# In-place transposes queued one tile later, a weight narrowing queued behind the exponentials, and the last keys' transposes queued behind the scores, in a fused attention and two-layer MLP kernel

## The chip, the core and the metric

The kernel runs on one core of a Trainium2 chip. The metric is the device time of one execution in microseconds (us); lower is better. The engines are TensorE (PE, with its weight loads shown apart as PEld), VectorE (DVE), ScalarE (ACT), GpSimd (POOL) and SyncE (SP), whose queue here issues almost all DMAs. Each engine works through one queue of instructions in the order in which they stand in it.

## What is computed

```python
# attention: q, k, v are 4 x 8 x 576 x 64 (batch, heads, positions, head size), float32
q_rot, k_rot = rotate(q), rotate(k)                    # rotary embedding
scores = matmul(q_rot, k_rot.T) / sqrt(64)
attn = exp(scores - max(scores))
attn = attn / (sum(attn) + 1e-9)
x = matmul(attn, v)                                    # -> 2304 x 512
# first layer, d_ff 768
h = maximum(maximum(x @ w1, x @ w2), x @ w3)
y = h @ w_out
# second layer, d_ff 2048
h2 = y @ w_in
out = (h2 * sigmoid(h2)) @ w_out2
```

The weights come as 64-bit floats, the rest as float32.

## The kernel before

The attention goes through 80 **tiles**, 20 for each of the four batches b. A tile is the key (b, hp, t): hp is one of four pairs of heads, and t one of five blocks of queries. Tiles with t from 0 to 3 hold 128 queries of both heads of the pair, tiles with t = 4 hold the last 64 queries of both heads on one set of 128 rows. A batch is taken in two halves: first t = 0, 1 for each pair, then t = 2, 3, 4.

For the tile of number j the loop in `attention()` writes down, in this order:

- `tile_scores(j)`: PE multiplies queries by keys into the one score buffer `s` (lines 394 to 404). There is a single such buffer, so the next tile's scores wait until this tile's exponentials have read it.
- `tile_max(j)`: DVE takes the negated row maximum `nb` (line 414), ACT the exponentials `e` with their sums (line 421).
- `tile_flip` of an earlier tile, from batch 1 on (line 491): DVE transposes 32 x 32 blocks of `pt` in place, once the DMAs of that tile have brought the exponentials there. I call this the flip.
- `av` (lines 532 and 536) for a group of two or three tiles whose flips are done: PE multiplies by v into `xp`, and ACT and DVE split the result into `x` (lines 539, 540).
- `tile_norm(j - 1)`: ACT passes the sums on (line 430), DVE takes reciprocals `rec` (line 431), ACT scales the exponentials (line 433).
- `tile_move(j - 1)`, from batch 1 on: SP issues four DMAs from `e` to `pt` (line 471).
- `tile_last(j - 2)`, from batch 1 on: PE transposes the last keys' columns of `e` (lines 438, 439, 481), which ACT and DVE copy out. Batch 0 makes all its transposes on PE in `tile_turn` and has neither moves nor flips.

Beside each tile other work is written down. The first layer, `moe1`, is paced by `x_ready`: PE multiplies x by w1, w2, w3 and then by w_out (line 623) into two PSUM buffers `m`, which ACT and DVE empty (lines 639, 641, 647, 648, 665). The rotary steps of the next batch run on POOL (lines 330 to 334). And `narrow_w2` brings the second layer's weights from 64 to 32 bits in 64 pieces: SP loads piece n (line 805) into one of three `z64` buffers; `narrow_a` takes it one step later, on ACT (line 214) and on POOL (line 216); `narrow_b` takes both results on DVE (lines 225, 226), one step later again; then ACT measures the piece (line 140) and SP stores it (line 781). Beside it, and mostly in the later part of this stretch, `prep_w8` loads stored pieces again (line 912), combines them on POOL (line 888) and splits them on ACT and DVE (lines 892, 896).

What stands in an engine's queue, and in which order, is settled when the program is built: a scheduler lays the instructions of each engine out by times that it reckons for them, and `tc.issue_after(x)` ties the instructions traced inside it behind instruction x, if they are on x's engine. On another engine the tie does nothing. `last["max"]` is the newest row maximum, on DVE; `exps[-1]` the newest exponential, on ACT.

Of the kernel before, what the change touches and what calls it, by code (L numbers as in the profile page):

```python
# [17 lines left out]
P = 128  # L18
# [4 lines left out]
def fused_kernel(  # L23
# [22 lines left out]
    nc = tc.nc  # L46
# [37 lines left out]
    ident = const.tile([P, P], F32, name="ident")  # L84
# [164 lines left out]
    last = {}  # L249
# [87 lines left out]
    def moved(b):  # L337
        return b > 0
# [41 lines left out]
    s_t, e_t, sum_t, pt_t, exps = {}, {}, {}, {}, []  # L380
# [3 lines left out]
    def both(s, o, step, n):  # L384

        return bass.AP(tensor=s.tensor, offset=s.offset + o, ap=[list(s.ap[0]), [step, 2], [1, n]])
    evacs = [0]

    def tile_scores(key):
        b, hp, t = key  # L390
        T, K, Q = T_t[b, hp]
        s = ps_s.tile([P, 1536], F32, tag="s", name="s")
        if t == 4:
            nc.tensor.matmul(s[:, 0:512], Q, T[:, 512:1024], start=True, stop=True)
            nc.tensor.matmul(s[:, 512:576], Q, T[:, 1024:1088], start=True, stop=True)
            s_t[key] = s
            return
        n = P
        qs = T[:, t * P:t * P + n]
        kt = T[:, 512:1024]  # L400
        nc.tensor.matmul(both(s, 512, 448, 64), qs, K, start=True, stop=True)  # L401
        for g, o in ((0, 0), (1, 1024)):
            r = slice(64 * g, 64 * g + 64)
            last["s"] = nc.tensor.matmul(s[:, o:o + 512], qs[r], kt[r], start=True, stop=True).ins  # L404
        s_t[key] = s

    def heads(key):
# [27 lines left out]
    def turn_last(e, to):  # L435

        tr = ps_t.tile([P, 512], F32, tag="tr", name="tr")
        nc.tensor.transpose(tr[:, 0:P], e[:, 448:576], ident)
        nc.tensor.transpose(tr[0:64, P:2 * P], e[:, 512:576], ident)
        to = to.rearrange("p (i q) -> p i q", i=2)  # L440
        t4 = tr[:, 0:2 * P].rearrange("p (a q i g) -> p a g i q", a=2, g=2, i=2)
        nc.scalar.activation(out=to[0:64], in_=t4[0:64, 1, 0], func=AF.Copy)
        nc.vector.tensor_copy(out=to[64:128], in_=t4[64:128, 0, 1])
# [29 lines left out]
    def tile_last(key):  # L473

        e = e_t.pop(key)
        pt, o = pt_of(key)
        to = blocks(pt)[1]
        if key[2] == 4:
            return turn_last(e, to[:, o:o + 64])
        tr = ps_t.tile([P, 512], F32, tag="tr", name="tr")  # L480
        nc.tensor.transpose(tr[:, 0:P], e[:, 512:640], ident)
        nc.scalar.activation(
            out=to[:, o:o + P].rearrange("p (i q) -> p i q", i=4), in_=tr[:, 0:P].rearrange("p (q i) -> p i q", i=4), func=AF.Copy
        )

    def tile_flip(key):

        pt, o = pt_of(key)
        n = 2 if key[2] == 4 else 4
        x = blocks(pt)[0][:, o // 32:o // 32 + n].rearrange("p i c k -> p (i c k)")  # L490
        nc.vector.transpose(out=x, in_=x)  # L491

    def tile_turn(key):
        b, hp, t = key
# [55 lines left out]
    tiles, events, first, x_ready, av_at = [], {}, {}, {}, {}  # L550

    def at(j, f, *a):
        events.setdefault(j, []).append((f, a))

    for b, hp, r in order:
        first.setdefault((b, hp), len(tiles))
        tiles += [(b, hp, t) for t in PARTS[r][2]]
        av_at.setdefault(len(tiles) + (3 if moved(b) else 2), []).append((b, hp, r))
        x_ready[b, r] = len(tiles) + (5 if moved(b) else 4)
    for i, (b, hp) in enumerate(pairs):  # L560
        u = first[b, hp]
        if b > 1:
            j = first[b, 0] + 3 * hp - 7
# [10 lines left out]
    for b in range(1, B):  # L574
        u = first[b, 0]
        for hp in range(NP):
            at(u - 10 + hp if hp < 2 else u - 3, load_v, b, hp)
            at(u - 6 + hp + hp // 2 * 2, v_max, b, hp)
        at(u, v_scale, b)

    def attention():

        back = lambda j, n: tiles[j - n] if n <= j < len(tiles) + n else None
        for j in range(len(tiles) + 5):
            if j < len(tiles):
                tile_scores(tiles[j])
                tile_max(tiles[j])
            key = back(j, 3)
            if key and moved(key[0]):
                tile_flip(key)  # L590
            for a in av_at.pop(j, ()):
                av(*a)
            key = back(j, 1)
            if key:
                tile_norm(key)
                if moved(key[0]):
                    tile_move(key)
            key = back(j, 2)
            if key:
                (tile_last if moved(key[0]) else tile_turn)(key)  # L600
            for f, a in events.pop(j, ()):
                f(*a)
            yield
# [165 lines left out]
    def narrow_w2(W, src, nm):  # L769

        part = {}
        M = W.m * 512 // 256
        for n in range(M + 4):
            if n >= 4:
                W.measure(n - 4)
                if nm == "wi":
                    i, o = divmod(n - 4, 2)
                    q, c = divmod(i, KC)  # L780
                    nc.sync.dma_start(
                        out=zscr[nm].rearrange("p (f c n) -> p f c n", c=KC, n=P)[:, 4 * q + 2 * o:4 * q + 2 * o + 2, c],
                        in_=W.t[n - 4].rearrange("p (f n) -> p f n", n=P),
                    )
                else:
                    nc.sync.dma_start(out=zscr[nm][:, (n - 4) * 256:(n - 3) * 256], in_=W.t[n - 4])
            if 2 <= n <= M + 1:
                with tc.issue_after(last["max"]):
                    W.narrow_b(n - 2, part.pop(n - 2, None))
            if 1 <= n <= M:  # L790
                if wide:
                    W.t[n - 1] = z_p.tile([P, 256], F32, tag="z", name="z")
                with tc.issue_after(last["max"]):
                    W.narrow_a(n - 1, part.get(n - 1), pool=True)
            if n < M:
                i, o = divmod(n * 256, 512)
                if nm == "wi":
                    q, c = divmod(i, KC)
                    from_ = src[c * P:(c + 1) * P, q * 512 + o:q * 512 + o + 256]
                else:  # L800
                    from_ = src[i * P:(i + 1) * P, o:o + 256]
                if wide:
                    part[n] = z64_p.tile([P, 256], w1.dtype, tag="z64", name="z64")
                    with tc.issue_after(last["load"]):
                        nc.sync.dma_start(out=part[n], in_=from_)
                else:
                    W.t[n] = z_p.tile([P, 256], F32, tag="z", name="z")
                    nc.sync.dma_start(out=W.t[n], in_=from_)
            yield
        W.scale("s" + nm, n=M)  # L810
        yield
# [572 lines left out]
```

## Time and profile before

| | us |
|---|---|
| median of 3 runs | 1084.35 (1081.48 to 1087.41) |
| profiled execution | 1086.89 |
| its span, first to last instruction | 1085.1 |
| PE busy | 941.8 (87%) |
| DVE busy | 690.9 (64%) |
| ACT busy | 606.9 (56%) |
| POOL busy | 493.3 (45%) |

The profile lists for each group of instructions how long it was busy, how long its engine stood idle just before it, and what ended that idle time. Busy shares are means over stages: batch 0's attention (to 165 us), attention of batches 1 to 3 beside the first layer (165 to 675), the end of the first layer (to some 740), and the second layer.

### The profile page before, as it was taken

To read this page: it belongs to the slowest core of one execution; us is meant where nothing else is said; L and a number is where in the kernel's file an instruction comes from. 1 tells how busy PE (TensorE), PEld (TensorE's weight loads), DVE (VectorE), ACT (ScalarE), POOL (GpSimd) and SP (SyncE) were. 2 spreads that over 40 slices of the span, in tenths; PEclk is the share of its full clock that TensorE was granted. 3 is DMA by queue.
4 is the path that set the end of the run, shared out by engine and by line. 5 is a ranking of instruction groups with operands and counts; after the bars stand their busy time and mean duration, and the time that the engine had idled before them with its cause. 6 is when DMAs were issued, how large, how long until landed. Compare 5 with 4: busy or idle time off the path is not lost. (4 is left out here: it accounts for less than half of the span.)

```text
span 1085.1 us, 19113 instructions
## 1 busy us (share of the span) xinstructions
PE 941.8 (87%) x6802; PEld 678.6 (63%) x6802; DVE 690.9 (64%) x1231; ACT 606.9 (56%) x1381; POOL 493.3 (45%) x548
## 2 busy tenths in 40 slices
PE   4677998888877978877978878999999899999998
PEld 2343664554554544454554446768888788888887
DVE  5658888544567544576655664576478677666554
ACT  3778686534665654566665654355455455545442
POOL 6734694850335600163132220276358646647254
PEclk9687998899999999998999898999999999999999
DMA  6833146755777855678677874635445234433201
GB/s 158 254 110 97 40 123 110 166 102 99 170 143 155 170 108 90 145 195 214 153 183 165 179 190 69 196 116 183 141 145 176 88 122 141 122 123 122 69 21 40
DMA packets 185198, 146.29 MB, mean 135 GB/s; under 512 B 51216, under 2 KB 168720, under 8 KB 185104
## 3 DMA queue, kind: packets, MB, share of 16 engines
q1 hardware_dynamic: 183600, 144.36, 53.5%
q8 instruction: 54, 0.88, 0.4%
q10 hardware_dynamic: 1504, 0.72, 0.2%
q14 instruction: 40, 0.33, 0.1%
HBM read 90.51 MB, written 26.21 MB: 108 GB/s over the span
## 5 line engine op out<-in xcount | busy, mean ns | idle before, releaser
L623 PE MATMUL m<-x,w 128*128 128x256 f16 (+1 forms) x1388 | 208.9, 300 | 23.0 <-DVE t L641 14.7
L623 PEld LDWEIGHTS <-w 128*128 128x128 f16 x1632 | 162.8, 102 | 100.9 <-issue 53.2
L216 POOL TENSOR_SCALAR z<-z 128x256 uint16<-128x256 uint16 x64 | 51.5, 804 | 242.0 <-ACT z L214 232.8
L491 DVE STREAM_TRANSPOSE pt<-pt 128x1024 f32<-128x1024 f32 (+1 forms) x60 | 68.2, 1137 | 140.5 <-DMA pt<-e 140.4
L1110 PEld LDWEIGHTS <-g 128*128 128x128 f16 x1485 | 146.1, 98 | 17.6
L1047 PEld LDWEIGHTS <-w8s 128*128 128x128 f16 x1344 | 131.1, 98 | 16.1 <-issue 0.9
L421 ACT ACTIVATE e<-s,nb 128x576 f32<-128x576 f32 x144 | 105.0, 734 | 54.7 <-DVE nb L414 53.7
L433 ACT ACTIVATE e<-e,rec 128x576 f32<-128x576 f32 x144 | 104.1, 766 | 53.1 <-DVE rec L431 52.8
L888 POOL TENSOR_TENSOR z<-z 128x128 f32<-128x128 f32 (+1 forms) x96 | 63.3, 677 | 102.1 <-PE m L120 46.3
L414 DVE TENSOR_REDUCE nb<-s 128x2 f32<-128x1152 f32 (+1 forms) x80 | 98.2, 1227 | 15.4 <-PE s L404 14.6
L536 PE MATMUL xp<-pt,vd 128*64 128x256 f32 (+1 forms) x512 | 83.0, 422 | 6.0 <-DVE pt L491 3.4
L404 PE MATMUL s<-T 64*128 64x512 f32 x256 | 84.4, 740 | 0.0
L1061 POOL TENSOR_TENSOR z<-t 128x256 f32<-128x256 f32 x32 | 27.1, 847 | 88.9 <-DVE t L1053 54.0
L623 PE MATMUL m<-h,wo 128*128 128x256 f16 (+1 forms) x448 | 66.0, 294 | 1.6 <-DVE wo L163 1.5
L214 ACT ACTIVATE z<-z 128x256 f32<-128x256 f32 x64 | 27.5, 431 | 69.3 <-DMA z<-in_moe_w_out_dram 41.8
L623 PEld LDWEIGHTS <-wo 128*128 128x128 f16 x512 | 50.6, 100 | 22.9 <-issue 8.0
L999 DVE SCALAR_TENSOR_TENSOR g<-gsum,sg,g 128x1024 f16<-128x1024 f32 x36 | 49.1, 1372 | 23.7 <-ACT g L998 23.3
L536 PEld LDWEIGHTS xp<-pt,vd 128*64 128x64 f32 x512 | 35.8, 138 | 41.5 <-issue 14.7
L998 ACT ACTIVATE g<-gsum,sg 128x1024 f16<-128x1024 f32 x36 | 40.8, 1141 | 36.9 <-POOL gsum L994 36.9
L330 POOL TENSOR_TENSOR w<-qk,sin_sb 128x384 f32<-128x384 f32 (+1 forms) x44 | 45.5, 1057 | 20.0 <-DMA qk<-in_q_dram 10.3
L401 PE MATMUL s<-kd,T 128*128 128x128 f32 x128 | 31.1, 329 | 23.4 <-ACT e L421 21.7
L1110 PE MATMUL c<-w,g 128*128 128x256 f16 x376 | 48.9, 277 | 0.0
(248 smaller groups left out, 1978.4 us busy)
## 6 DMA issues: line engine op xcount, KB each, us to landing
w8s<-w8scr SPq DMA_DIRECT2D x64, 448.0 KB, 4.4
pt<-e SPq DMA_DIRECT2D x192, 128.0 KB, 3.9
z<-in_moe_w_in_dram SPq DMA_DIRECT2D x32, 256.0 KB, 3.7
z<-in_moe_w_out_dram SPq DMA_DIRECT2D x32, 256.0 KB, 3.5
w<-in_moe_w_dram SPq DMA_DIRECT2D x6, 768.0 KB, 6.5
wo<-in_moe_w_dram SPq DMA_DIRECT2D x6, 768.0 KB, 4.8
qk<-in_q_dram SPq DMA_DIRECT2D x32, 128.0 KB, 3.8
vd<-in_v_dram SPq DMA_DIRECT2D x16, 256.0 KB, 3.2
```

What stands on the lines that cost most here:

```text
L216: nc.gpsimd.tensor_scalar(out=q[:, :, 2], in0=q[:, :, 1], scalar1=step, scalar2=off, op0=ALU.mult, op1=ALU.add)
L404: last["s"] = nc.tensor.matmul(s[:, o:o + 512], qs[r], kt[r], start=True, stop=True).ins
L414: x = nc.vector.tensor_reduce(out=nb[:, 0:m], in_=both(s, 0, 960, 576) if m > 1 else s[:, 0:576], op=ALU.max, axis=AX.X, negate=True)
L421: x = nc.scalar.activation(out=e[:, HK[g]], in_=s[:, SK[g]], func=AF.Exp, bias=nb[:, g:g + 1], accum_out=sm[:, g:g + 1])
L433: nc.scalar.activation(out=e[:, HK[g]], in_=e[:, HK[g]], func=AF.Copy, scale=r[:, g:g + 1])
L491: nc.vector.transpose(out=x, in_=x)
L536: nc.tensor.matmul(xp[r, 0:n], v4[:, g, c, :], turned(c, g), start=False, stop=(c == 3))
L623: nc.tensor.matmul(ps[:, 0:n], l, r, start=(first and i == 0), stop=(not more and i == len(passes) - 1))
L888: nc.gpsimd.tensor_tensor(out=z[:, o], in0=z[:, x], in1=z[:, y], op=op)
L999: nc.vector.scalar_tensor_tensor(out=l, in0=x, scalar=sg_t[jb], in1=h, op0=ALU.mult, op1=ALU.subtract)
L1047: nc.tensor.matmul(o, l, r, start=(i == 0), stop=(i == len(passes) - 1))
L1110: x = nc.tensor.matmul(ps, l, r, start=first, stop=last_, skip_group_check=True)
```

## The change

- The flip is tied behind `last["max"]`, and it is written down for tile j - 2 instead of j - 3. As it is traced after `tile_max(j)`, that is the maximum of the second next tile.
- `narrow_a` in `narrow_w2` is tied behind `exps[-1]`. Before, it named `last["max"]`, a DVE instruction, which ties nothing on ACT or POOL.
- PE's transposes of the last keys are tied behind the newest score matmul, now kept in `last["score"]`.
- The moved batches lose the extra step: `av` is written down two steps behind its last tile instead of three, `x_ready` is four instead of five, and the loop ends a step earlier. The loads of v for two head pairs go one step earlier.

```diff
@@ tile_scores
-            nc.tensor.matmul(s[:, 512:576], Q, T[:, 1024:1088], start=True, stop=True)
+            last["score"] = nc.tensor.matmul(s[:, 512:576], Q, T[:, 1024:1088], start=True, stop=True).ins
...
-            last["s"] = nc.tensor.matmul(s[:, o:o + 512], qs[r], kt[r], start=True, stop=True).ins
+            last["s"] = last["score"] = nc.tensor.matmul(s[:, o:o + 512], qs[r], kt[r], start=True, stop=True).ins
@@ turn_last
-        nc.tensor.transpose(tr[:, 0:P], e[:, 448:576], ident)
-        nc.tensor.transpose(tr[0:64, P:2 * P], e[:, 512:576], ident)
+        with tc.issue_after(last["score"]):
+            nc.tensor.transpose(tr[:, 0:P], e[:, 448:576], ident)
+            nc.tensor.transpose(tr[0:64, P:2 * P], e[:, 512:576], ident)
@@ tile_last
-        nc.tensor.transpose(tr[:, 0:P], e[:, 512:640], ident)
+        with tc.issue_after(last["score"]):
+            nc.tensor.transpose(tr[:, 0:P], e[:, 512:640], ident)
@@ tile_flip
-        nc.vector.transpose(out=x, in_=x)
+        with tc.issue_after(last["max"]):
+            nc.vector.transpose(out=x, in_=x)
@@
-        av_at.setdefault(len(tiles) + (3 if moved(b) else 2), []).append((b, hp, r))
-        x_ready[b, r] = len(tiles) + (5 if moved(b) else 4)
+        av_at.setdefault(len(tiles) + 2, []).append((b, hp, r))
+        x_ready[b, r] = len(tiles) + 4
...
-            at(u - 10 + hp if hp < 2 else u - 3, load_v, b, hp)
+            at(u - 10 + hp if hp < 2 else u - 4, load_v, b, hp)
@@ attention
-        for j in range(len(tiles) + 5):
+        for j in range(len(tiles) + 4):
...
-            key = back(j, 3)
+            key = back(j, 2)
@@ narrow_w2
-                with tc.issue_after(last["max"]):
+                with tc.issue_after(exps[-1]):
                     W.narrow_a(n - 1, part.get(n - 1), pool=True)
```

The first place is DVE's queue in batch 1, from the maximum of tile 29 (counted from 0) to that of tile 30, whose line has only one pair of results less (128x1). Before, the rows are these; the flip of `pt` is that of tile 28, and `rec_2498` is tile 29's reciprocal.

```order
L414 TENSOR_REDUCE nb_2399<-s_2395 128x2
L225 TENSOR_SCALAR z_2357<-z_2357 128x256
L491 STREAM_TRANSPOSE pt_2423<-pt_2423 128x1024
L226 SCALAR_TENSOR_TENSOR z_2357<-z_0_2287,z_2357 128x256
L641 SCALAR_TENSOR_TENSOR t_2469<-m_2456,t_2454 128x320
L540 SCALAR_TENSOR_TENSOR x_2094<-xp_2544,vs_1706,x_2094 128x256
L431 RECIPROCAL rec_2498<-rec_2498 128x2
L414 TENSOR_REDUCE nb_2492<-s_2489 128x1
```

In the changed program the same two maxima are followed by these rows of DVE; the first flip is tile 27's, the second tile 28's, and `rec_2511` is tile 29's reciprocal.

```order
L414 TENSOR_REDUCE nb_2412<-s_2408 128x2
L494 STREAM_TRANSPOSE pt_2262<-pt_2262 128x1024
L225 TENSOR_SCALAR z_2370<-z_2370 128x256
L644 SCALAR_TENSOR_TENSOR t_2388<-m_2375,t_2321 128x320
L226 SCALAR_TENSOR_TENSOR z_2370<-z_0_2288,z_2370 128x256
L644 SCALAR_TENSOR_TENSOR t_2403<-m_2390,t_2388 128x320
L431 RECIPROCAL rec_2511<-rec_2511 128x2
L651 TENSOR_TENSOR h_2_2405<-t_2403,h_2_2405 128x320
L543 SCALAR_TENSOR_TENSOR x_2029<-xp_2499,vs_1706,x_2029 128x256
L414 TENSOR_REDUCE nb_2493<-s_2490 128x1
L494 STREAM_TRANSPOSE pt_2424<-pt_2424 128x1024
```

Tile 28's flip has moved from between tile 29's maximum and tile 29's reciprocal to directly behind tile 30's maximum, with tile 29's reciprocal ahead of it. Over the program, 57 of the 60 flips stood behind the maximum of the next tile (3 behind their own), 40 of them ahead of that next tile's reciprocal; in the changed program 58 of 60 stand behind the maximum of the second next tile and all of these behind the next tile's reciprocal.

The second place is ACT's queue at tiles 29 and 30, where line 214 is `narrow_a`. Before, from tile 29's exponentials on:

```order
L421 ACTIVATE e_2401,sm_2402<-s_2395,nb_2399 128x576 x2
L639 ACTIVATE t_2454<-m_2441 128x320
L482 ACTIVATE pt_2423<-tr_2507 128x128
L539 ACTIVATE x_2094<-xp_2544,vs_1706 128x256
L430 ACTIVATE rec_2498<-sm_2402 128x2
L140 ACTIVATE junk_2577,wi2m_297<-z_2357 128x256
L433 ACTIVATE e_2401<-e_2401,rec_2498 128x576 x2
L214 ACTIVATE z_2582<-z_0_2531 128x256
L421 ACTIVATE e_2494,sm_2495<-s_2489,nb_2492 128x576
```

And in the changed program:

```order
L421 ACTIVATE e_2414,sm_2415<-s_2408,nb_2412 128x576 x2
L214 ACTIVATE z_2437<-z_1_2373 128x256
L430 ACTIVATE rec_2511<-sm_2415 128x2
L140 ACTIVATE junk_2578,wi2m_297<-z_2370 128x256
L650 ACTIVATE h_2_2405<-t_2403 128x320
L433 ACTIVATE e_2414<-e_2414,rec_2511 128x576 x2
L542 ACTIVATE x_2029<-xp_2499,vs_1706 128x256
L421 ACTIVATE e_2495,sm_2496<-s_2490,nb_2493 128x576
```

The narrowing has moved from just ahead of the next tile's exponentials to just behind this tile's, and the piece it takes there is an earlier one (the piece in buffer `z_0` of the first listing is taken two tiles later now). Its loads on SP stay between the moves of the same tiles, and `narrow_b` on DVE stays within a tile of where it stood. So for 9 of the 64 pieces `narrow_b` now stands in DVE's queue behind the maximum of the very tile behind whose exponentials its `narrow_a` stands, and for the others one tile later; before, it was mostly two or three tiles later. PE's transposes of the last keys stood mostly ahead of the scores of the second next tile and stand behind them now. No instruction of these stages is added or dropped, and `av` moves by at most two tiles.

## Rows read from the trace of the kernel before

**Rows 1.** Windows: us, busy PE, PEld, DVE, ACT, POOL (x), PEclk, DMA share, GB/s.

```profile
100.00:165.00 65.00, 59.08 (x396) 39.92 (x395) 52.85 (x98) 46.87 (x119) 47.17 (x42) 0.93 0.24 69
165.00:675.00 510.00, 419.24 (x2586) 255.99 (x2587) 302.84 (x574) 299.96 (x826) 167.80 (x212) 0.94 0.70 149
```

**Rows 2.** Waits of all engines, 165 to 675 us: total us, times, longest.

```profile
POOL z L216 <- ACT z L214: 232.8, 44, 27.9
DVE pt L491 <- DMA pt<-e: 140.4, 52, 6.0
...
ACT e L433 <- DVE rec L431: 50.4, 30, 5.5
ACT e L421 <- DVE nb L414: 47.0, 25, 5.2
ACT z L214 <- DMA z<-in_moe_w_out_dram: 41.8, 22, 4.2
POOL z L888 <- DMA z<-zwi: 27.2, 11, 9.4
...
ACT z L214 <- DMA z<-in_moe_w_in_dram: 26.8, 11, 4.9
```

**Rows 3.** Waits of PE alone, 165 to 675 us.

```profile
PE m L623 <- DVE t L641: 27.1, 17, 3.6
PE s L401 <- ACT e L421: 17.8, 12, 4.0
PE m L623 <- ACT y L665: 6.5, 3, 3.4
...
PE tr L481 <- ACT e L433: 3.4, 3, 2.3
...
PE xp L536 <- DVE pt L491: 3.4, 2, 2.0
```

**Rows 4.** Timeline around two flips: start, us, engine, line, [idle before <-releaser].

```profile
256.68 0.33 PE L395 MATMUL s<-T,qd 128*128 128x64 f32 x2
258.21 1.25 DVE L491 STREAM_TRANSPOSE pt<-pt 128x1024 f32<-128x1024 f32 x1 [3.94 <-DMA pt<-e]
...
260.22 0.43 PE L623 MATMUL m<-h,wo1f 128*128 128x320 f16 x2 [1.58 <-DVE t L641]
...
260.55 0.73 DVE L414 TENSOR_REDUCE nb<-s 128x1 f32<-128x576 f32 x1
260.66 1.44 ACT L433 ACTIVATE e<-e,rec 128x576 f32<-128x576 f32 x2 [0.35 <-DVE rec L431]
262.13 2.61 SPq L471 DMA_DIRECT2D pt<-e  x4
...
268.26 1.25 DVE L491 STREAM_TRANSPOSE pt<-pt 128x1024 f32<-128x1024 f32 x1 [2.94 <-DMA pt<-e]
268.91 0.43 ACT L214 ACTIVATE z<-z 128x256 f32<-128x256 f32 x1 [2.77 <-DMA z<-in_moe_w_in_dram]
...
269.81 0.43 PE L623 MATMUL m<-h,wo1f 128*128 128x320 f16 x2 [2.42 <-ACT y L665]
```

**Rows 5.** Groups by line, 165 to 675 us: count, busy us, mean ns, idle before.

```profile
L421 ACT ACTIVATE e<-s,nb 128x576 f32<-128x576 f32 x108 | 78.7, 733 | 48.0 <-DVE nb L414 47.0 <-DMA zwo<-z 0.8
...
L491 DVE STREAM_TRANSPOSE pt<-pt 128x1024 f32<-128x1024 f32 (+1 forms) x60 | 68.2, 1137 | 140.5 <-DMA pt<-e 140.4
...
L216 POOL TENSOR_SCALAR z<-z 128x256 uint16<-128x256 uint16 x61 | 48.8, 801 | 241.7 <-ACT z L214 232.8 <-DMA qk<-in_q_dram 6.5 <-DVE kd L374 1.1
...
L214 ACT ACTIVATE z<-z 128x256 f32<-128x256 f32 x61 | 26.1, 430 | 68.8 <-DMA z<-in_moe_w_out_dram 41.8 <-DMA z<-in_moe_w_in_dram 26.8
```

**Rows 6.** Line 226 over the run: duration ns min/median/max, first and last start.

```profile
L226 DVE SCALAR_TENSOR_TENSOR z<-z,z x64: 382/425/1219, 180.7 to 644.2; 128x256 int32<-128x256 int32 x64
```

**Rows 7.** Timeline of one narrowing step beside the rotary work on POOL.

```profile
215.63 2.18 POOL L334 TENSOR_TENSOR qk<-qk,w 128x384 f32<-128x384 f32 x2
215.93 1.03 DVE L226 SCALAR_TENSOR_TENSOR z<-z,z 128x256 int32<-128x256 int32 x1
```

## The prediction

> **What bounds the kernel now.** I read the busy times by stretch first. Between 165 and 675 us, where batches 1 to 3 go through the attention beside the first layer, PE works 419.24 of 510 us; just before, between 100 and 165 us, where batch 0 does the same without moves and flips, it works 59.08 of 65 us, 0.909 of the time, at nearly the same granted clock (0.93 against 0.94) [rows 1]. So 90.8 us of PE time stand idle in the long stretch, and no engine is full there: DVE has 302.84, ACT 299.96, POOL 167.80 [rows 1]. It is a stretch of waits. The change touches nothing in the second layer behind it, so all that can be won lies in these 91 us and in the clock.
>
> Next the waits. The largest that is not POOL waiting for its own input is DVE's: 140.4 us in 52 waits in front of flips, for the DMAs that bring `pt` [rows 2]. ACT waits 50.4 us for reciprocals and 47.0 us for maxima, both DVE's, and 41.8 + 26.8 = 68.6 us in front of `narrow_a` for weight loads [rows 2]. PE's own waits name the results of these two engines: 27.1 us for `t` out of DVE, 17.8 us for exponentials, 6.5 us for `y`, 3.4 us for scaled exponentials, 3.4 us for flips, together 58 us of the 91 [rows 3].
>
> The timeline shows how the one becomes the other. A score matmul ends at 257.0 us, yet its maximum starts at 260.55, because DVE's queue holds a flip that has waited 3.94 us and starts at 258.21; the reciprocal behind it lets ACT scale only at 260.66, and PE stands 1.58 us until 260.22 for a `t` that DVE could not empty earlier [rows 4]. Ten microseconds on, a flip waits 2.94 us and `narrow_a` 2.77 us on ACT, and PE loses 2.42 us behind ACT's `y` [rows 4]. Of 3.94 + 2.94 + 2.77 = 9.65 us of such waits PE lost 4.00, a factor of 0.41.
>
> **The change part by part.**
>
> *The flip.* Its DMAs are issued at 262.13, right behind the scaling that starts at 260.66 and takes 1.44, and the flip starts at 268.26 [rows 4]: 6.1 us. Before, it stands behind the maximum of the next tile and mostly in front of that tile's reciprocal, so DVE reaches it too early by a mean of 140.4 / 60 = 2.3 us, at worst 6.0 [rows 2]. In the second listing it stands behind one more maximum. A tile takes 510 / 60 = 8.5 us, the 60 flips standing in that stretch [rows 1, 5]; even if a tile shrank to 7 us, the worst wait of 6.0 us would be covered. I take the whole 140.4 us of DVE waiting as removed; the bounds are all and half of it. What is late next: `av` follows the flip, one maximum later, but it moves by two tiles at most and the first layer's pieces behind it have a step of slack written down as before. PE waits for flips only 3.4 us now [rows 3]. The `pt` buffers are two, and the first move of the group after next comes more than a tile after `av`. I cost this at nothing; uncovered it would be the flip itself, 1.14 us [rows 5], for each of the 24 groups, 27 us.
>
> *`narrow_a`.* It leaves the place in front of the next exponentials, where ACT waited 68.6 us for loads, and comes one to two tiles after that. Its loads keep their place on SP. At most 4.9 us were missing [rows 2], less than a tile, so I take all of this away; at worst it stays. Its own 0.43 us [rows 5] now stand between exponentials and sums instead of a place or two later on ACT, ahead of the next exponentials both times: nothing. What it costs: for 9 pieces DVE reaches `narrow_b` in the same tile. From the end of the maximum, two exponentials (2 x 0.733), 0.43 on ACT and 0.80 on POOL make 2.70 us, of which DVE spends 1.14 on the flip [rows 5]: 1.56 us each, 14 us of DVE, times 0.41 = 6 us. For the other 55 a tile lies between; bounds below.
>
> *The last keys' transposes.* PE waited 3.4 us in front of them for scaled exponentials [rows 3]; behind one more score matmul these are there. It is counted in the 58 us. Three `e` buffers stand, and the fourth tile's exponentials come a tile after these transposes: nothing, or at most what ACT waits for PE then, which has no row; I leave up to 5 us in the range.
>
> *One step less, loads of v earlier.* The end of the stretch is the same chain of flip, `av` and first layer; no work is removed. A tile may be won at the end or none; I take none.
>
> *The sum.* Two ways. By density: at batch 0's 0.909, 419.24 us of PE work take 461 us instead of 510, a gain of 49. By waits: 0.41 x (140.4 + 68.6) = 86 us, more than the 58 us that PE's waits name, so 58 at most; if only half of those go, 29. The density lies between, and I take it less the 6 us of the same-tile narrowing: 49 - 6 = 43 us. The profiled execution took 1086.9 us (a span of 1085.1 and 1.8 around it), which gives 1043.9; the median of the runs stands 2.5 us lower, at 1084.35, which gives **1041 us**.
>
> The clock is left out of the sum. It was 0.94 granted while PE stood idle 91 of 510 us [rows 1]; 1.00 would take up to 0.06 x 419 = 25 us more off, but batch 0's stretch had 0.93 at the denser rate. Some of these 25 us go into the low end.
>
> **The rivals.**
>
> *DVE waits for POOL in place of the DMAs.* `narrow_a` comes later, `narrow_b` does not, so the two or three tiles between them shrink to one. POOL works in order: it had been free when ACT's half of the step arrived in 44 of 64 cases [rows 2], and in the others it stood in rotary steps of 1.09 us each [rows 7] or in the combination, which waited 27.2 us for loads, 9.4 at worst [rows 2]. If DVE took over those 27.2 us, 11 us of PE time go; with the low end of the waits, 29 - 6 - 11 = 12 us remain: 1072. Against it: a tile of 8 us covers most. Chance 0.15 for something between 1058 and 1072.
>
> *Moves still land late.* A shorter stretch carries the same bytes: the DMA share of 0.70 [rows 1] becomes 0.70 x 510 / 467 = 0.76. If half the flip's wait returned, 70 x 0.41 = 29 us go: 1070. Chance 0.05.
>
> *DVE and POOL get in each other's way.* Line 226 takes 0.425 us at the median and 1.219 at most [rows 6]; one of 1.03 us ran beside a rotary step on POOL [rows 7]. If all 64 took the longest, DVE spends 64 x 0.8 = 51 us more, times 0.41 = 21: 1062. Chance 0.04; the moved steps meet POOL at new moments, not more often. The Trainium skill (SBUF — State Buffer, "Who interferes with whom") states a rule by which this would happen: a VectorE instruction with two inputs in SBUF and a GpSimd instruction that reads SBUF use one read interface, and the one that starts second waits for the other's end. By that rule, with which the long row agrees, a denser DVE meets POOL more often, which speaks against the change: the sum would be 1062 if every piece met a POOL step, and 1041 if the meetings stay as they are.
>
> *The stretch does not shorten.* If PE's idle time were set by its two PSUM buffers and the single score buffer whatever DVE does, waits would only change their names. 33 of the 91 us are outside the 58. Against it: batch 0, with the same buffers, stands idle only 9%. Time 1079 to 1089, chance 0.07.
>
> *Slower.* The same narrowing, but deciding: DVE stands in front of `narrow_b` in every tile, and the reciprocal and the next maximum are queued behind it, as they were behind the flip. It decides from 209 / 64 = 3.3 us a piece on. If the 20 pieces that found POOL occupied each waited through a run of nine rotary steps, 9.8 us, and the 9 same-tile pieces 1.56, with the 27.2 us of the combination, that makes 196 + 14 + 27 = 237 us against 209: 28 x 0.41 = 11 us slower, 1095. The listings put `narrow_b` late enough for most, so 0.05.
>
> **How the numbers follow.** The forecast has 0.64, within 1015 to 1058: the low end is the density's 49 us and 20 us of the clock, the high end the low waits, 29, less a few. The two rivals that cost part of it and the port take 0.24, mostly up to 1072. The range of 1015 to 1072 leaves out no change, slower, and a little on both sides. A measurement of this kernel tells about 0.5%, 5.4 us, from no change. Faster: 0.64 + 0.15 + 0.05 + 0.04 = 0.88; same 0.07; slower 0.05.
>
> **What would show it.** In the changed profile the flips' wait for DMAs falls from 140 us to under 20, `narrow_a`'s for loads from 69 to under 15, ACT's waits for reciprocals and maxima shrink by more than half, and PE's share between the first flip and the last rises from 0.82 to about 0.90, with the second layer as long as before. The forecast is wrong if DVE's idle time in front of `narrow_b` (lines 225 and 226) exceeds 30 us, if the flip still waits, or if PE's wait for `t` stays at 27 us although DVE no longer waits for DMAs.

## The result, and the profile after

The changed kernel takes 997.23 us at the median (995.05 to 1000.13, 4 runs). Beside it the kernel before takes 1082.91, so the ratio is 0.9205, with a 95% interval of 0.9166 to 0.9244: 86 us faster, twice the 43 us that were forecast, and 18 us below the low end of the range. The profiled execution takes 997.75 us, 89.1 less than the one of before (1086.9).

First the page's busy times of the changed kernel.

```profile
span 996.0 us, 19123 instructions
PE 912.6 (92%) x6802; PEld 671.5 (67%) x6802; DVE 698.1 (70%) x1231; ACT 604.4 (61%) x1381; POOL 494.0 (50%) x548
```

Then the stretches of the changed kernel, in the columns of [rows 1]. The long one ends with the last flip again, which is at 585 us now and was at 675.

```profile
100.00:165.00 65.00, 60.27 (x400) 40.70 (x399) 51.97 (x100) 46.29 (x117) 43.87 (x39) 0.93 0.24 68
...
165.00:585.00 420.00, 386.31 (x2548) 244.79 (x2548) 306.07 (x568) 297.04 (x823) 172.42 (x215) 0.98 0.85 181
585.00:996.00 411.00, 401.92 (x3574) 349.59 (x3573) 268.62 (x445) 195.75 (x302) 220.37 (x233) 0.99 0.37 119
```

The rest behind the last flip takes 411 us; before it ran from 675 to 1085, 410 us. So the whole gain lies in the stretch, 510 to 420 us. It has two parts. PE's idle time went from 90.8 to 420 - 386.31 = 33.7 us, 57 less. And PE's busy time went from 419.24 to 386.31, 33 less, while the granted clock rose from 0.94 to 0.98. A few of these 33 us are work that now stands behind the last flip: the window lists 2548 matmuls instead of 2586. Over the whole run, with 6802 matmuls in both kernels, PE is busy 912.6 us instead of 941.8, 29 less for the same work. DVE and ACT do what they did before, 306 and 297 us, in 90 us less.

The waits of all engines in the changed kernel, 165 to 585 us (total us, times, longest), answer to [rows 2].

```profile
POOL z L216 <- ACT z L214: 77.8, 13, 31.7
POOL z L891 <- DMA z<-zwi: 56.8, 15, 11.3
ACT e L421 <- DVE nb L414: 30.0, 34, 1.9
...
DVE pt L494 <- DMA pt<-e: 15.6, 12, 3.0
...
DVE z L226 <- POOL z L216: 11.6, 8, 4.4
```

The flip's wait, 140.4 us in 52 cases, is 15.6 in 12. ACT's waits for maxima fell less, from 47.0 to 30.0 us, but none is longer than 1.9 us now, where one of 5.2 stood before. DVE waits for POOL 11.6 us in front of line 226, where it stood idle 1.1 us in all before; it is the wait of the narrowing that now follows itself within a tile (e8 below, which undoes that, has none there). POOL's wait for its loads (line 891, the combination) doubled, from 27.2 to 56.8 us, and POOL has 172 us of work in 420: PE's waits name it nowhere.

PE's own waits in the changed kernel answer to [rows 3].

```profile
PE s L401 <- ACT e L421: 8.8, 7, 1.6
PE s L394 <- ACT e L421: 6.8, 5, 3.8
PE m L626 <- DVE t L644: 6.0, 5, 1.6
...
PE m L626 <- ACT y L668: 1.7, 2, 1.2
...
PE xp L539 <- DVE pt L494: 0.5, 2, 0.3
```

The 27.1 us for `t` out of DVE are 6.0, and those for flips went from 3.4 to 0.5, although each flip stands behind one more maximum.

Four of the changed kernel's groups, 165 to 587 us, answer to [rows 5].

```profile
L433 ACT ACTIVATE e<-e,rec 128x576 f32<-128x576 f32 x108 | 78.3, 768 | 7.1 <-DVE rec L431 7.0
...
L494 DVE STREAM_TRANSPOSE pt<-pt 128x1024 f32<-128x1024 f32 (+1 forms) x60 | 67.8, 1130 | 16.2 <-DMA pt<-e 15.6 <-issue 0.4
...
L226 DVE SCALAR_TENSOR_TENSOR z<-z,z 128x256 int32<-128x256 int32 x64 | 33.9, 530 | 12.8 <-POOL z L216 11.6 <-issue 0.4
...
L214 ACT ACTIVATE z<-z 128x256 f32<-128x256 f32 x64 | 27.0, 435 | 9.7 <-DMA z<-in_moe_w_in_dram 5.4 <-DMA z<-in_moe_w_out_dram 4.3
```

`narrow_a` (line 214) waits 9.7 us for loads where it waited 68.6, and the scaling (line 433) 7.0 us for reciprocals where it waited 50.4. The durations of flip and scaling are those of before.

The timeline of the changed kernel where a tile's scores end and a flip follows, as in [rows 4]:

```profile
254.82 0.33 PE L395 MATMUL s<-T,qd 128*128 128x64 f32 x2
...
255.22 0.74 DVE L414 TENSOR_REDUCE nb<-s 128x1 f32<-128x576 f32 x1
...
255.89 1.23 DVE L494 STREAM_TRANSPOSE pt<-pt 128x1024 f32<-128x1024 f32 x1
256.00 0.74 ACT L421 ACTIVATE e<-s,nb 128x576 f32<-128x576 f32 x1 [1.89 <-DVE nb L414]
...
256.74 0.43 ACT L214 ACTIVATE z<-z 128x256 f32<-128x256 f32 x1
...
257.49 0.78 ACT L433 ACTIVATE e<-e,rec 128x576 f32<-128x576 f32 x1 [0.23 <-DVE rec L431]
```

The maximum starts 0.07 us behind the scores' end at 255.15, where it came 3.5 us late before, because no flip stands ahead of it. The flip behind it starts at once, with no idle time in front of it; ACT takes the exponentials 0.04 us after the maximum's end and the narrowing right behind them, 0.74 + 0.43 us, without a wait.

### The profile page after: what moved, and what is told of

Same layout as the page of the kernel before. It is cut to its first block, busy times and chain, and to the rows that moved or that the text cites. A ratio compares the mean times of both kernels' runs of the same rounds, so it can differ in the third digit from the quotient of the medians.

```text
span 996.0 us, 19123 instructions
## 1 busy us (share of the span) xinstructions
PE 912.6 (92%) x6802; PEld 671.5 (67%) x6802; DVE 698.1 (70%) x1231; ACT 604.4 (61%) x1381; POOL 494.0 (50%) x548
## 4 chain that ended last, share of the span: by engine, by line
PE 37%; DMA 7%; DVE 4%; ACT 2%; POOL 2%; issue 2%; SPq 1%; DVEq 0%; ACTq 0%; POOLq 0%
PE m L1050 8%; PE mb L1050 6%; PE c L1113 4%; PE a L1113 4%; PE b L1113 4%; PE mg L626 3%; PE m L626 3%; PE d L1113 2%; DMA w8scr<-z 2%; POOL gsum L997 1%; DMA w8s<-w8scr 1%; DMA pt<-e 1%; PE m L1018 1%; PE mb L1018 1%; PE m L1113 1%
## 5 line engine op out<-in xcount | busy, mean ns | idle before, releaser
L626 PE MATMUL m<-x,w 128*128 128x256 f16 (+1 forms) x1388 | 193.7, 289 | 11.1 <-ACT t L642 4.3
L626 PEld LDWEIGHTS <-w 128*128 128x128 f16 x1632 | 160.7, 99 | 62.9 <-issue 19.0
L891 POOL TENSOR_TENSOR z<-z 128x128 f32<-128x128 f32 (+1 forms) x96 | 61.7, 660 | 134.5 <-DMA z<-zwi 56.8
L216 POOL TENSOR_SCALAR z<-z 128x256 uint16<-128x256 uint16 x64 | 54.1, 845 | 105.9 <-ACT z L214 77.8
L404 PE MATMUL s<-T 64*128 64x512 f32 x256 | 81.1, 695 | 0.0
L494 DVE STREAM_TRANSPOSE pt<-pt 128x1024 f32<-128x1024 f32 (+1 forms) x60 | 67.8, 1130 | 16.2 <-DMA pt<-e 15.6
L539 PE MATMUL xp<-pt,vd 128*64 128x256 f32 (+1 forms) x512 | 76.5, 415 | 0.5 <-DVE pt L494 0.5
L1064 POOL TENSOR_TENSOR z<-t 128x256 f32<-128x256 f32 x32 | 27.1, 847 | 89.2 <-DVE t L1056 54.1
L330 POOL TENSOR_TENSOR w<-qk,sin_sb 128x384 f32<-128x384 f32 (+1 forms) x44 | 46.0, 1065 | 35.4 <-DMA qk<-in_q_dram 24.0
L626 PE MATMUL m<-h,wo 128*128 128x256 f16 (+1 forms) x448 | 60.8, 286 | 0.1
L539 PEld LDWEIGHTS xp<-pt,vd 128*64 128x64 f32 x512 | 35.3, 138 | 36.5 <-issue 13.3
L644 DVE SCALAR_TENSOR_TENSOR t<-m,t 128x256 f32<-128x256 f32 (+1 forms) x82 | 36.7, 447 | 18.9 <-PE m L626 11.6
L1113 PE MATMUL b<-w,g 128*128 128x256 f16 x376 | 48.5, 273 | 0.0
```

Source lines behind the costliest of these rows:

```text
L216: nc.gpsimd.tensor_scalar(out=q[:, :, 2], in0=q[:, :, 1], scalar1=step, scalar2=off, op0=ALU.mult, op1=ALU.add)
L404: last["s"] = last["score"] = nc.tensor.matmul(s[:, o:o + 512], qs[r], kt[r], start=True, stop=True).ins
L539: nc.tensor.matmul(xp[r, 0:n], v4[:, g, c, :], turned(c, g), start=False, stop=(c == 3))
L626: nc.tensor.matmul(ps[:, 0:n], l, r, start=(first and i == 0), stop=(not more and i == len(passes) - 1))
L891: nc.gpsimd.tensor_tensor(out=z[:, o], in0=z[:, x], in1=z[:, y], op=op)
L1113: x = nc.tensor.matmul(ps, l, r, start=first, stop=last_, skip_group_check=True)
```

## The experiments

"Gain" is (1 - ratio) x 1083.9, the median of the kernel before as it was measured beside e1 to e4; beside the others it was within 1 us of that. The last columns are for the stretch from 165 us to the last flip: its length, PE's idle time in it, its granted clock, DVE's wait for moves (in front of flips) and ACT's for loads (in front of `narrow_a`).

| kernel | median us | ratio [95%] | gain | stretch | PE idle | clock | moves | loads |
|---|---|---|---|---|---|---|---|---|
| before | - | 1 | 0 | 510 | 90.8 | 0.94 | 140.4 | 68.6 |
| e3_turn_alone | 1079.71 | 0.9969 [0.9949, 0.9988] | 3 | 503 | 78.6 | 0.92 | 122.2 | 65.9 |
| e2_narrow_alone | 1074.93 | 0.9917 [0.9895, 0.9939] | 9 | 501 | 79.8 | 0.92 | 143.1 | 2.1 |
| e4_without_flip_tie | 1072.1 | 0.9899 [0.9874, 0.9923] | 11 | 504 | 82.1 | 0.93 | 142.5 | 0.8 |
| e11_flip_tied_in_batch_2 | 1069.02 | 0.9882 [0.9848, 0.9917] | 13 | 493 | 77.0 | 0.94 | 89.3 | 62.4 |
| e10_flip_behind_reciprocal | 1017.46 | 0.9399 [0.9368, 0.9429] | 65 | 446 | 44.4 | 0.96 | 69.4 | 2.6 |
| e5_without_narrow_tie | 1014.57 | 0.9372 [0.934, 0.9405] | 68 | 441 | 48.1 | 0.96 | 15.8 | 74.9 |
| e1_flip_alone | 1013.73 | 0.9365 [0.9338, 0.9392] | 69 | 433 | 41.5 | 0.98 | 8.4 | 77.1 |
| e8_narrow_b_later | 1005.53 | 0.9273 [0.9252, 0.9293] | 79 | 427 | 40.5 | 0.97 | 14.5 | 31.9 |
| e9_flip_third_next | 1001.74 | 0.9264 [0.9221, 0.9308] | 80 | 423 | 27.4 | 0.98 | 4.3 | 15.8 |
| e6_without_turn_tie | 1001.04 | 0.9235 [0.9214, 0.9256] | 83 | 424 | 36.5 | 0.98 | 25.8 | 9.8 |
| e7_without_earlier_step | 999.67 | 0.9225 [0.92, 0.925] | 84 | 421 | 30.6 | 0.98 | 30.9 | 8.7 |
| changed | 997.23 | 0.9205 [0.9166, 0.9244] | 86 | 420 | 33.7 | 0.98 | 15.6 | 9.7 |

**One part alone, put into the kernel before.** The flip with its tie, two tiles behind:

```
-        nc.vector.transpose(out=x, in_=x)
+        with tc.issue_after(last["max"]):
+            nc.vector.transpose(out=x, in_=x)
...
-            key = back(j, 3)
+            key = back(j, 2)
```

> The kernel before with the flip alone tied behind the second next tile's maximum; the narrowing, the transposes on PE, av and the steps as before. If the flip's wait in front of the reciprocal is the main cause, its 140 us of DVE waiting fall under 20 and about two thirds of the 86 us go: 1020 to 1030. If the waits hide each other and only both together help: 1045 to 1060, with ACT's wait for weight loads grown above 69 us. If the step less is what helps: 1075 or more.

Measured: 1013.73 us, a gain of 69, most of the change and more than the 1020 to 1030 expected. The windows and waits of this kernel:

```profile
165.00:598.00 433.00, 391.52 (x2547) 246.53 (x2547) 303.14 (x565) 297.42 (x820) 166.48 (x212) 0.98 0.80 176
```

```profile
ACT z L214 <- DMA z<-in_moe_w_out_dram: 43.4, 26, 5.0
...
ACT z L214 <- DMA z<-in_moe_w_in_dram: 33.7, 22, 4.6
...
ACT e L421 <- DVE nb L414: 13.6, 13, 1.9
```

The flip's wait is gone, 8.4 us, and ACT's for maxima with it, 13.6. The clock is already 0.98. What is late next is `narrow_a`: the loads' wait grew from 68.6 to 43.4 + 33.7 = 77.1 us, likely since the tiles that the loads have are shorter.

The narrowing alone:

```
-                with tc.issue_after(last["max"]):
+                with tc.issue_after(exps[-1]):
                     W.narrow_a(n - 1, part.get(n - 1), pool=True)
```

> The kernel before with narrow_a alone tied behind the exponentials. If each wait pays for itself, ACT's 69 us in front of narrow_a fall under 15 and about a quarter goes: 1055 to 1068. If the flip's wait covers this one, the time stays within 1075 to 1085 and DVE's wait for flips grows above 140 us.

Measured: 1074.93 us, a gain of 9, at the edge of the second case, whose sign came too: DVE's wait for flips is above 140 us. Its waits:

```profile
DVE pt L491 <- DMA pt<-e: 143.1, 52, 5.8
...
ACT e L421 <- DVE nb L414: 77.2, 37, 7.8
...
ACT e L433 <- DVE rec L431: 62.5, 26, 5.3
```

ACT's 68.6 us for loads are 2.1, but its waits for maxima grew from 47.0 to 77.2 and for reciprocals from 50.4 to 62.5, together 42 us. The waits in front of `narrow_a` covered waits for DVE, and DVE still stands 143 us in front of flips. So ACT's wait was largely a second one, in the shadow of DVE's: ACT would have had to wait there anyway.

The last keys' turns alone:

```
+            last["score"] = nc.tensor.matmul(s[:, 512:576], Q, T[:, 1024:1088], start=True, stop=True).ins
...
+        with tc.issue_after(last["score"]):
             nc.tensor.transpose(tr[:, 0:P], e[:, 448:576], ident)
```

> The kernel before with the last keys' transposes alone tied behind the scores. PE waited only 3.4 us in front of them: 1078 to 1085 if PE's own waits tell what such a tie is worth; 1060 or less if these transposes, queued ahead of the scores, held the scores up without showing it.

Measured: 1079.71 us, a gain of 3, as expected from PE's own waits: no more than executions of the kernel before differ among themselves (1083.23 to 1086.19 us beside this one). Taken out of the changed kernel, below, the same edit is worth 3 us as well. The three alone make 69 + 9 + 3 = 81 of 86 us, so they nearly add up.

**One part taken out of the change.** The flip without its tie (it stays written two tiles behind, and stands behind the next tile's maximum for 53 of 60):

```
-        with tc.issue_after(last["max"]):
-            nc.vector.transpose(out=x, in_=x)
+        nc.vector.transpose(out=x, in_=x)
```

> The changed kernel without the flip's tie: it is written down a tile earlier than before, and the built order puts 53 of 60 flips behind the next tile's maximum again. If the flip is the main cause: 1050 to 1065, with 120 us or more of DVE waiting for moves. If the other parts carry the gain: under 1020.

Measured: 1072.1 us, above the 1050 to 1065 expected. The waits of this kernel:

```profile
DVE pt L493 <- DMA pt<-e: 142.5, 48, 6.6
ACT e L421 <- DVE nb L414: 67.2, 33, 7.6
...
ACT e L433 <- DVE rec L431: 56.5, 29, 5.2
```

The tie is worth 86 - 11 = 75 us beside the other parts. The 11 us that are left are what the narrowing and the turns gave alone, 9 + 3, so the step from three tiles to two without the tie is worth nothing that shows: DVE waits 142.5 us for moves, as in the kernel before.

The narrowing tied to the maximum again:

```
-                with tc.issue_after(exps[-1]):
+                with tc.issue_after(last["max"]):
```

> The changed kernel with narrow_a untied as before. If ACT's wait in front of narrow_a has a price of its own beside the flip's: 1010 to 1025, with 50 us or more of ACT waiting for weight loads. If the flip alone carries the gain: 995 to 1003.

Measured: 1014.57 us, in the first case's range, so the tie is worth 18 us here, twice its 9 alone. With DVE punctual, ACT's 74.9 us for loads are no longer in a shadow: PE waits 21.6 us for exponentials in front of line 401, against 8.8 in the changed kernel.

The turns without their tie, and the earlier step undone:

```
-        with tc.issue_after(last["score"]):
-            nc.tensor.transpose(tr[:, 0:P], e[:, 448:576], ident)
+        nc.tensor.transpose(tr[:, 0:P], e[:, 448:576], ident)
```

> The changed kernel with the last keys' transposes untied as before. By PE's own wait of 3.4 us: 997 to 1002. If the transposes hold the scores up once the other waits are gone: 1008 or more, with PE waiting for scaled exponentials.

```
-        av_at.setdefault(len(tiles) + 2, []).append((b, hp, r))
-        x_ready[b, r] = len(tiles) + 4
+        av_at.setdefault(len(tiles) + (3 if moved(b) else 2), []).append((b, hp, r))
+        x_ready[b, r] = len(tiles) + (5 if moved(b) else 4)
...
-        for j in range(len(tiles) + 4):
+        for j in range(len(tiles) + 5):
```

> The changed kernel with av, the first layer's readiness, the loop's length and the loads of v as before; the flip stays tied behind the second next maximum. If the step less is worth nothing but a tile at the end: 995 to 1005. If the earlier av and first layer are part of the gain: 1015 or more.

Measured: 1001.04 and 999.67 us, both in their first range, ratios of 0.9235 and 0.9225 whose intervals overlap the change's own. Neither edit can be told from nothing in these runs: by the ratios they are worth 3 and 2 us, and the intervals allow up to some 8.

**Why the tie helps, the reciprocal or the maximum?** The tie puts the flip behind two things: the next tile's reciprocal, and the second next tile's maximum. Tied to the reciprocal alone, it stands behind the reciprocal (59 of 60) but mostly ahead of that maximum. For such a tie `tile_norm` and `tile_move` of tile j - 1 have to be written down ahead of the flip and of `av`, so these move too:

```
+        last["rec"] = nc.vector.reciprocal(out=r[:, 0:m], in_=r[:, 0:m]).ins
...
-        with tc.issue_after(last["max"]):
+        with tc.issue_after(last["rec"]):
             nc.vector.transpose(out=x, in_=x)
...
+            key = back(j, 1)
+            if key:
+                tile_norm(key)
+                if moved(key[0]):
+                    tile_move(key)
             key = back(j, 2)
...
```

> The changed kernel with the flip tied behind the next tile's reciprocal in place of the second next tile's maximum: 55 of 60 flips stand between that reciprocal and the second next maximum. If the harm came from the reciprocal queued behind the flip: 998 to 1012, and what DVE still waits there costs little. If the flip must clear the second next maximum as well, because its DMAs land that late: 1020 to 1050, with over 70 us of DVE waiting for moves and ACT waiting for maxima, not for reciprocals.

Measured: 1017.46 us, between the two ranges. Its waits:

```profile
ACT e L421 <- DVE nb L414: 69.8, 46, 4.1
DVE pt L494 <- DMA pt<-e: 69.4, 39, 3.8
...
ACT e L433 <- DVE rec L431: 6.9, 18, 1.2
```

Against the kernel without the tie, the reciprocals' wait is gone, 56.5 us there and 6.9 here. Half of the flip's wait is still there, 69.4 of 142.5 us, and maxima are delayed as before, 69.8 us against 67.2. By ratio, of the tie's 75 us (0.9899 to 0.9205) the step behind the reciprocal gives 0.9899 - 0.9399 = 0.050, 54 us, and the step behind the maximum the other 0.0194, 21 us. The first step does two things at once, which no run parts: the reciprocal no longer stands behind the flip, and the flip is reached later.

A likely reason why the reciprocal counts for so much stands in [rows 4]. A reciprocal queued behind a waiting flip delays the scaling, the scaling delays the moves, and these are what the next flip waits for. From the flip at 258.21 us by way of reciprocal, scaling and moves to the flip at 268.26 this round takes 10.05 us, more than the 8.5 us of a mean tile. Before, 40 of 60 flips stood ahead of the next tile's reciprocal. That this round set the pace is argued from one place of the timeline and not shown by a run of its own.

**What the change costs.** Two experiments push the changed kernel further. In one, `narrow_b` comes a tile later, so that DVE need not wait for POOL; in the other the flip comes one tile later still. First `narrow_b`:

```
-            if 2 <= n <= M + 1:
+            if 3 <= n <= M + 2:
...
-                    W.narrow_b(n - 2, part.pop(n - 2, None))
+                    W.narrow_b(n - 3, part.pop(n - 3, None))
```

> The changed kernel with narrow_b written down one step later, so that none stands in the tile of its narrow_a. DVE waited 11.6 us for POOL in front of line 226. If that wait is on the path: 990 to 995. If it is covered: 995 to 999. If the later release of the 64-bit buffers holds SP's queue up, so that loads and moves come late: 1003 or more, with ACT or DVE waiting for loads or moves.

Measured: 1005.53 us, the third case, slower than the change by 0.9273 - 0.9205 = 0.0068, 7 us, with intervals that do not touch. DVE's wait for POOL in front of line 226 is gone. The buffers of the pieces are held a tile longer, and the loads come later, a likely cause that was not tested apart. Its waits in front of `narrow_a`:

```profile
ACT z L214 <- DMA z<-in_moe_w_in_dram: 17.2, 12, 3.0
...
ACT z L214 <- DMA z<-in_moe_w_out_dram: 14.7, 10, 2.5
```

That is 31.9 us instead of 9.7, more than the 11.6 us that DVE could win.

Then the flip:

```
-            key = back(j, 2)
+            key = back(j, 3)
```

with the steps of `av`, `x_ready`, `load_v` and the loop as in the kernel before.

> The changed kernel with the flip, av and the first layer's readiness one step later: 57 of 60 flips stand behind the third next tile's maximum. If the rest of the flips' wait (15.6 us) still costs: 990 to 995, with no wait left. If it is covered, or av one tile later eats what is won: 996 to 1004. If pt's two buffers are now held too long: 1010 or more, with SP's moves waiting for PE.

Measured: 1001.74 us, in the second case's range. The flip's wait falls to 4.3 us (57 of 60 stand behind the third next maximum), and no time is won. The nearest kernel is e7, which has the same steps of `av` and of the first layer: from e7 to this one the flip's wait falls from 30.9 to 4.3 us, with ratios of 0.9225 and 0.9264 whose intervals overlap. But DVE's wait for POOL grows from 10.0 to 18.9 us and ACT's for loads from 8.7 to 15.8. So what is left of the flip's wait has no price that shows, though other waits may have taken what it gave.

**Density or clock?** The flip tied in batch 2 alone, with batches 1 and 3 as before:

```
+        with tc.issue_after(last["max"]) if key[0] == 2 else nullcontext():
             nc.vector.transpose(out=x, in_=x)
...
+            for n in (2, 3):
+                key = back(j, n)
+                if key and moved(key[0]) and n == (2 if key[0] == 2 else 3):
+                    tile_flip(key)
```

> The kernel before with the flips of batch 2 alone tied and written a step earlier. If the clock and PE's idle time follow the flips' wait from place to place: about a third of the 70 us that the flip alone gave, 1056 to 1064; batch 2's stretch some 20 to 28 us shorter, with its clock at 0.97 or more and PE's busy time for the same work about a tenth lower than in batches 1 and 3, whose clock stays at 0.92 to 0.95. If the clock rises only once the whole stretch is dense: batch 2's clock stays near 0.94 and the gain is 10 to 17 us.

Measured: 1069.02 us, 13 less than before, the number of the second case. The windows list time, busy times, clock and DMA in the columns of [rows 1]. Batches 2 and 3, first in the kernel before:

```profile
341.00:506.00 165.00, 132.81 (x824) 80.67 (x824) 98.44 (x187) 97.59 (x270) 53.98 (x66) 0.96 0.69 152
506.00:663.00 157.00, 132.64 (x789) 79.28 (x790) 96.28 (x185) 99.35 (x265) 36.60 (x60) 0.92 0.74 170
```

and in this one, with six short windows inside batch 2 around one gap of PE:

```profile
338.00:483.00 145.00, 130.81 (x816) 80.84 (x817) 99.03 (x185) 97.76 (x270) 52.89 (x66) 0.94 0.75 169
483.00:648.00 165.00, 135.37 (x808) 80.61 (x807) 98.14 (x188) 100.17 (x269) 36.35 (x60) 0.92 0.72 163
...
383.00:385.50 2.50, 1.91 (x15) 1.18 (x13) 0.00 (x0) 0.67 (x2) 0.16 (x1) 1.00 0.96 117
385.50:388.00 2.50, 0.00 (x0) 0.00 (x0) 2.35 (x3) 0.68 (x2) 0.60 (x1) 0.81 0.03 6
388.00:390.50 2.50, 1.46 (x4) 1.01 (x6) 2.03 (x6) 2.50 (x11) 0.00 (x0) 0.50 0.04 10
390.50:393.00 2.50, 2.50 (x9) 0.72 (x6) 1.10 (x1) 1.32 (x3) 0.00 (x0) 0.50 0.47 148
393.00:395.50 2.50, 2.50 (x16) 1.64 (x14) 2.38 (x6) 2.05 (x6) 0.76 (x1) 0.83 1.03 167
395.50:398.00 2.50, 2.50 (x22) 1.64 (x22) 1.20 (x7) 1.61 (x5) 0.00 (x0) 1.00 1.10 192
```

Batch 2 is 20 us shorter, 18 of it idle time of PE (165 - 132.81 = 32.2 to 145 - 130.81 = 14.2). But its clock did not rise with the density: 0.94, against 0.96 before, in one execution each. Three gaps of PE, 4.45, 4.13 and 3.09 us, are left in this batch, and with each of them the clock falls to 0.50 and stays there for some microseconds of work; the short windows show the second. Batch 3, whose flips are not tied, became 8 us longer, 5 of it idle time of PE. Its longest gap shows the old harm once more: tile 61's flip waits 3.90 us for its moves and starts at 504.90 us, the maximum, the exponentials and a `t` of the first layer come behind it, and PE stands 7.39 us until 509.12.

## Why the prediction was wrong

The direction was right, and so was the path from a waiting flip over the queue of DVE to PE's idle time. The sum was too small by half. In the stretch it missed 90 - 43 = 47 us: 33 of them are PE's busy time, which it held fixed, 57 - 49 = 8 are idle time, and 6 were taken off for the narrowing.

- **The flip.** Right: the wait fell to 15.6 us, under the 20 forecast, PE hardly waits for flips (0.5 us), and the flip's tie is by far the largest part. That the reciprocal ahead matters more than the maximum ahead, 54 against 21 us, the prediction did not say.
- **`narrow_a`.** Its wait fell to 9.7 us, under the 15 forecast. Its place in the sum, 68.6 us beside the flip's 140.4 with one factor for both, was not right: alone it gives 9 us, since ACT would have waited for DVE anyway, and behind a punctual DVE 18.
- **The step that failed is the sum by density**, "419.24 us of PE work take 461 us instead of 510". Both of its terms were off. The larger miss is the work: it was held at 419.24 us and measured 386.31. The smaller is the density: batch 0's 0.909 was taken as what PE can reach, and PE reached 386.31 / 420 = 0.920. Nothing in the rows made batch 0 a ceiling: it runs without moves and flips, but also at another place of the first layer.
- **The bound by PE's waits** came near only by luck. The 57 us of idle time that came back look like the 58 that were named [rows 3], but of the five waits in that 58 there are 17 us left, so 41 came back there, and the other 16 came out of the 33 us that the prediction had left outside.
- **The clock was left out of the sum**, since batch 0 had 0.93 at a denser rate; its bound was 25 us. The mean granted clock of the whole profiled execution is 0.951 before and 0.969 after. With the lower level at half the clock that is a loss of at most 0.049 x 1085.1 = 53 us of PE time before and 0.031 x 996.0 = 31 us after: 22 us at most of the 29 that PE is busy less for the same work. The rest, some 7 us or more, is not settled. The first layer's matmuls show the clock at work:

```profile
L623 PE MATMUL m<-x,w 128*128 128x256 f16 x516 | 73.3, 291 | 6.6 <-DVE t L641 6.4
```

```profile
L626 PE MATMUL m<-x,w 128*128 128x256 f16 x485 | 60.8, 273 | 4.3 <-DVE t L644 2.1 <-ACT t L642 1.8 <-DVE ve L130 0.3
```

  Sorted by the clock granted at their start, the 446 of the kernel before that start at the full clock take 273 ns in the mean and the 70 at half of it 410; in the changed kernel all of them start at the full clock and take 273. So the fall of the mean from 291 to 273 ns is the clock.
- **What the clock is worth in time** is less than that, as far as the record tells. Executions of one kernel differ in clock by as much as the two kernels do: the eight of the kernel before beside e1 to e4 run from 0.940 (1086.19 us) to 0.958 (1083.42 us). A line fitted through all 71 recorded executions, each taken against the mean of its own kernel, gives as an estimate 2.7 us for each 0.01 of clock (standard error 0.6), so about 5 us for 0.018. Work done at the lower clock seems to be covered in part by waits that are there anyway. No kernel moved the clock by itself, so its part of the 86 us stays open, between some 5 and 22.
- **The narrowing's same-tile wait**, 6 us off the sum, measured 11.6 us of DVE's time, 12.8 with the rest in front of line 226, under the 30 that would have refuted the forecast. e8, which takes the same-tile order away, won nothing, but it delays loads as well, so no run shows its price by itself.
- **The turns and the earlier step**, counted at nothing or inside the 58: 3 and 2 us, which can't be told from nothing.
- **Other signs.** PE's share rose from 0.82 to 0.92 (about 0.90 forecast), the rest behind stayed as long, PE's wait for `t` fell to 6.0 us. ACT's wait for reciprocals shrank by 86%, but that for maxima by 36%, not by half as forecast: what is left, 34 waits of at most 1.9 us, is of the size of a maximum itself (1.23 us in the mean), which stands between scores and exponentials anyway.

Of the rivals, DVE waiting for POOL appeared as a wait, 11.6 us, under half of the 27.2 that it was priced at, and the time of 1058 to 1072 that went with it did not. Moves landing late did not come: the DMA share rose to 0.85, over the 0.76 worked out, and DVE waits for moves only 15.6 us. A stretch that doesn't shorten, and a slower kernel, fell with the measured time. The port rival fell by its own row. Line 226 in the changed kernel, in the columns of [rows 6]:

```profile
L226 DVE SCALAR_TENSOR_TENSOR z<-z,z x64: 380/425/1216, 177.6 to 557.8; 128x256 int32<-128x256 int32 x64
```

The median is 425 ns as before and the longest 1216 in place of 1219, and the mean fell from 568 to 530, though DVE is denser by a fifth (306 of 420 us against 303 of 510). The Trainium skill's rule on the shared read interface (SBUF — State Buffer, "Who interferes with whom") may explain the long ones; that a denser DVE meets POOL more often, which the prediction drew from it, no run here shows.

## What to carry to other kernels

An instruction that waits at the head of an in-order queue is charged to everybody behind it: put it behind the short ones whose results another engine awaits (here the reciprocal first, worth 54 us, then the next maximum, 21), even if it then starts later itself. When you price such a change, don't take the density of some other stretch as a ceiling (49 us against the 57 of idle time that came back), and don't hold the bounding engine's busy time fixed: here it fell by 33 us. A sum that fits can still be luck, so look whether the waits that it names are the ones that went. Of two engines that wait in turn, the wait in the shadow of the other is worth little until the other is gone: 9 us alone, 18 after.

## What the hardware showed

The mean idle share of PE in a stretch does not tell its granted clock. In e11's batch 2 PE was busy 0.90 of the time and had 0.94; in the same batch before it was busy 0.80 and had 0.96, in one execution each. The timeline of PE in e11's batch 2 shows what a gap costs behind its end:

```profile
389.04 0.80 PE L401 MATMUL s<-kd,T 128*128 128x128 f32 x2 [4.13 <-ACT e L421]
389.77 2.08 PE L404 MATMUL s<-T 64*128 64x512 f32 x4
391.78 2.81 PE L625 MATMUL m<-x,w 128*128 128x320 f16 x12
```

The four score matmuls take 2.08 us at the granted 0.50 (1.2 of 2.4 GHz); in the same kernel, at 261 us, four take 1.13. PE has been idle 4.13 us ahead of them. In the stretch PE has 20 gaps over 2 us in the kernel before and 4 in the changed one, and the clock's mean is 0.94 and 0.98. But the number of such gaps does not tell the clock either: e2 and e3 have 12 and 15 of them, with less idle time than before, and 0.92. What decides is not settled here. The Trainium skill (TensorE: Matmul & The Clock Gate, "HAM oscillation — how this bites in real kernels") describes a matmul kernel that falls to the lower clock behind each of its waits. This trace agrees for the gap of 4.13 us and the windows around it; it does not show it for every wait, as batch 2 before, with eight gaps over 2 us, had 0.96.
